# Forward attention scores as rows: q stationary in four column groups, K^T streamed 512 wide, softmax on rows, P transposed back

## The chip, the cores and the metric

The kernel runs on one core of a Trainium2 chip. The metric is device time in microseconds (us) of one execution; lower is better. The kernel before takes 2199 us (median of three executions, 2189 to 2205).

Names used below: PE is TensorE (matmuls), DVE is VectorE, ACT is ScalarE, POOL is GpSimd, PEld is the loading of stationary weights. PSUM is the memory that matmuls write, SBUF the working memory. The *granted clock* is the share of its full clock that PE had, as the profile records it. A *chunk* is eight transposed blocks of K, the content of one PSUM buffer. A *pair* is two heads of the attention that are worked on together. There are 128 heads (batch 4 times 32 heads), so 64 pairs.

## The reference, cut to what matters

A decode step of one attention block and one gated MLP, forward and backward. The part that matters is the attention forward, over a cache of 4096 keys of 128 numbers for each head:

```python
q = (x @ wq).reshape(B, Sq, H, Dh)...              # one query row per head
scores = jnp.einsum("bhqd,bhkd->bhqk", q, k_cache) * (Dh ** -0.5)
p = softmax(scores, axis=-1)
o = jnp.einsum("bhqk,bhkd->bhqd", p, v_cache)
# ... then the MLP, then the gradients of everything
# (cut: layer norms, MLP, vjp)
```

## The kernel before

Everything that the change touches lies in one stage, the forward over K and V. The engine order of each instruction queue is fixed when the kernel is built: the builder takes the operations in the order of the program as priorities, but lets a later operation go ahead where its inputs and buffers are ready in the builder's own estimate. Each queue then runs in that built order.

For one head, K is loaded with 32 rows of keys on each partition, PE transposes its 32 blocks (eight to a PSUM buffer, from a pool of two buffers, `psT`), and ACT and DVE copy them to `KT`. The scores are 32 matmuls with a block of K^T stationary and one column of q moving, so that the scores of a head fill a 128x32 tile:

```python
        def S_head(gi, hl):
            # ... cut: load of Kn, KT tile
            transpose_blocks(psT, KT, Kn, ["s", "v", "s", "s"])     # 4 chunks of 8 blocks; second chunk copied by VectorE
            # ...
            for j in range(SJ):
                nc.tensor.matmul(S_ps[:, hl, j:j + 1], lhsT=KT[:, j, :], rhs=qT_bf[:, bh:bh + 1], start=True, stop=True)
            hold[gi]["K"].append(Kn)

        def softmax(gi):
            S_ps = hold[gi]["S"]                                     # 128 x (2 heads x 32)
            nc.vector.tensor_reduce(out=mx[:], in_=S_ps[:], axis=AX.X, op=ALU.max)
            nc.tensor.transpose(xps[0:G, 0:P], mx[:], ident_f[:])    # maximum over partitions ...
            nc.vector.tensor_reduce(out=gm[:], in_=xps[0:G, 0:P], axis=AX.X, op=ALU.max)
            # ... cut: dg, and a small matmul that sends -scale*max to all partitions (bps, nm)
            for hl in range(G):
                nc.scalar.activation(out=E[:, hl, :], in_=S_ps[:, hl, :], func=AF.Exp, bias=nm[:, hl:hl + 1],
                                     scale=scale, accum_out=rs[:, hl:hl + 1])
            # ... cut: sum over partitions by a matmul with ones (lps), rl = 1 / sum
            nc.vector.tensor_tensor(out=P_all[:, gi * G:(gi + 1) * G, :], in0=E[:],
                                    in1=rl[:, :, None].to_broadcast([P, G, SJ]), op=ALU.mult)

        def M_head(gi, hl):
            # ... cut: load of Vn; PK = P x K, one product of 128x4096 on VectorE
            for j in range(SJ):
                nc.tensor.matmul(M_ps[:], lhsT=Vn[:, j, :], rhs=PK[:, j, :], start=(j == 0), stop=(j == SJ - 1))
            for c in range(2):                                       # kP: sums of PK over the keys, in four column groups
                for q in range(4):
                    # ...
                    nc.tensor.matmul(kP_ps[32 * q:32 * (q + 1), :, :], lhsT=ones_window(w), rhs=PK[:, j0:j0 + 4, 0:Dh],
                                     start=..., stop=..., tile_position=(0, 32 * q))
            # ... cut

        for gi in range(NGI + 1):
            if gi < NGI:
                for hl in range(G):
                    S_head(gi, hl)
                softmax(gi)
            if gi > 0:
                for hl in range(G):
                    M_head(gi - 1, hl)
```

Of the kernel before, what the change touches and what calls it, by code (L numbers as in the profile page):

```python
# [14 lines left out]
G = 2  # L15
# [10 lines left out]
def kernel(  # L26
# [71 lines left out]
    nc.vector.tensor_copy(out=sel_f[:], in_=ident_f[:, 0:H])  # L98
    for q in range(1, P // H):
        nc.vector.tensor_tensor(out=sel_f[:], in0=sel_f[:], in1=ident_f[:, q * H:(q + 1) * H], op=ALU.add)  # L100
    onesw = []
    for i in range(2):
        t = const.tile([P, 64], BF16, name=f"onesw{i}")
# [75 lines left out]
    def transpose_blocks(psW, XT, Xn, engs):  # L179
        for g in range(NG):  # L180
            pt = psW.tile([P, GW, P], BF16, tag="tps", name="pt_tps")
            for i in range(GW):
                nc.tensor.transpose(pt[:, i, :], Xn[:, g * GW + i, :], ident_b[:])  # L183
            evac_copy(XT[:, g * GW:(g + 1) * GW, :], pt[:], eng=engs[g % len(engs)])
# [38 lines left out]

    with ExitStack() as c1:
        psT = c1.enter_context(tc.tile_pool(name="psT", bufs=2, space=bass.MemoryType.PSUM))
        psS = c1.enter_context(tc.tile_pool(name="psS", bufs=2, space=bass.MemoryType.PSUM))
        psM = c1.enter_context(tc.tile_pool(name="psM", bufs=2, space=bass.MemoryType.PSUM))
        psK = c1.enter_context(tc.tile_pool(name="psK", bufs=1, space=bass.MemoryType.PSUM))
        psX = c1.enter_context(tc.tile_pool(name="psX", bufs=1, space=bass.MemoryType.PSUM))
# [1 line left out]
        xtp = c1.enter_context(tc.tile_pool(name="xtp", bufs=XT_BUFS))  # L231
        vp = c1.enter_context(tc.tile_pool(name="vp", bufs=V_BUFS))
        pkp = c1.enter_context(tc.tile_pool(name="pkp", bufs=PK_BUFS))
        wop = c1.enter_context(tc.tile_pool(name="wop", bufs=2))
        kps = c1.enter_context(tc.tile_pool(name="kps", bufs=1))
        hold = {}

        def S_head(gi, hl):
            bh = gi * G + hl
            b, h = bh_of(bh)  # L240
            Kn = kp.tile([P, SJ, Dh], BF16, name="Kn", tag="Kn")
            nc.sync.dma_start(out=Kn[:], in_=rows_of(A_k_cache[b, h]))
            KT = xtp.tile([P, SJ, P], BF16, name="KT", tag="KT")
            transpose_blocks(psT, KT, Kn, ["s", "v", "s", "s"])
            if hl == 0:
                hold[gi] = {"S": psS.tile([P, G, SJ], FP32, name="S_ps", tag="S"), "K": []}
            S_ps = hold[gi]["S"]
            for j in range(SJ):
                nc.tensor.matmul(S_ps[:, hl, j:j + 1], lhsT=KT[:, j, :], rhs=qT_bf[:, bh:bh + 1], start=True, stop=True)  # L249
            hold[gi]["K"].append(Kn)  # L250

        def softmax(gi):
            S_ps = hold[gi]["S"]
            mx = small.tile([P, G], FP32, tag="mx", name="mx")
            nc.vector.tensor_reduce(out=mx[:], in_=S_ps[:], axis=AX.X, op=ALU.max)  # L255
            xps = psX.tile([P, 512], FP32, tag="x", name="x_ps")
            nc.tensor.transpose(xps[0:G, 0:P], mx[:], ident_f[:])
            gm = small.tile([G, 1], FP32, tag="gm", name="gm")
            nc.vector.tensor_reduce(out=gm[:], in_=xps[0:G, 0:P], axis=AX.X, op=ALU.max)
            dg = small.tile([G, G], FP32, tag="dg", name="dg")  # L260
            nc.vector.tensor_scalar(out=dg[:], in0=ident_f[0:G, 0:G], scalar1=gm[:], scalar2=-scale,
                                    op0=ALU.mult, op1=ALU.mult)
            bps = psX.tile([P, 512], FP32, tag="x", name="b_ps")
            nc.tensor.matmul(bps[:, 0:G], lhsT=ones_f[0:G, :], rhs=dg[:], start=True, stop=True)
            nm = small.tile([P, G], FP32, tag="nm", name="nm")
            nc.vector.tensor_copy(out=nm[:], in_=bps[:, 0:G])
            E = small.tile([P, G, SJ], FP32, tag="E", name="E")
            rs = small.tile([P, G], FP32, tag="rs", name="rs")
            for hl in range(G):
                nc.scalar.activation(out=E[:, hl, :], in_=S_ps[:, hl, :], func=AF.Exp, bias=nm[:, hl:hl + 1],  # L270
                                     scale=scale, accum_out=rs[:, hl:hl + 1])
            lps = psX.tile([P, 512], FP32, tag="x", name="l_ps")
            nc.tensor.matmul(lps[:, 0:G], lhsT=ones_f[:], rhs=rs[:], start=True, stop=True)
            rl = small.tile([P, G], FP32, tag="rl", name="rl")
            nc.vector.reciprocal(out=rl[:], in_=lps[:, 0:G])
            nc.vector.tensor_tensor(out=P_all[:, gi * G:(gi + 1) * G, :], in0=E[:],
                                    in1=rl[:, :, None].to_broadcast([P, G, SJ]), op=ALU.mult)

        def M_head(gi, hl):
            bh = gi * G + hl  # L280
# [23 lines left out]
                                     start=(w == 0 and c == 0), stop=(w == 31 and c == 1), tile_position=(0, 32 * q))  # L304
            nc.scalar.copy(out=M_all[:, bh, :], in_=M_ps[:, 0:Dh + 1])  # L305
            if w == 31:
                kP_sb = kps.tile([P, 4, Dh], FP32, name="kP_sb", tag="kP_sb")
                nc.scalar.copy(out=kP_sb[:], in_=kP_ps[:])
                kt_ps = psX.tile([P, 512], FP32, tag="x", name="kt_ps")
                for c in range(4):  # L310
                    nc.tensor.matmul(kt_ps[:, 0:H], lhsT=kP_sb[:, c, :], rhs=sel_f[:], start=(c == 0), stop=(c == 3))
                nc.vector.tensor_copy(out=kPT[:, bh - 31:bh + 1], in_=kt_ps[:, 0:H])
# [409 lines left out]
```

## Time and profile before

| stage | from, us | to, us | what it does |
|---|---|---|---|
| forward | 20 | 944 | 64 pairs: transposes of K, scores, softmax, products with K and V |
| middle | 944 | 1102 | MLP forward and backward, small weights |
| backward | 1102 | 2202 | gradients of the caches, bound by DMA |

The table is read from the windows view (busy time of each engine in a stretch). The forward takes 924 us. In it PE's busy share is 0.87, DVE's 0.53, ACT's 0.49, and DMA's 0.75, so that no engine is full.

### The profile page before, as it was taken

How to read it: one execution, taken by the hardware profiler on the slowest of the kernel's cores; microseconds unless marked ns; L12 is line 12 of the kernel's file. 1: busy time of each engine (PE TensorE's matmuls, PEld its weight loads, DVE VectorE, ACT ScalarE, POOL GpSimd, SP SyncE). 2: the span in 40 equal slices, each digit the busy share in tenths (PEclk: the TensorE clock that was granted, in tenths of full speed). 3: DMA queues.
4: the chain of work that ended last, by engine and by line, in shares of the span. 5: the costliest groups of instructions: out<-in, count | busy, mean ns of one | idle time of the engine just before them, and what ended most of it. 6: DMA issues, size and time to landing. Idle time of an engine off the chain costs nothing.

```text
span 2202.3 us, 52207 instructions
## 1 busy us (share of the span) xinstructions
PE 1603.6 (73%) x23496; PEld 1321.8 (60%) x23496; DVE 1156.5 (53%) x1431; ACT 1074.7 (49%) x1523; POOL 212.7 (10%) x433
## 2 busy tenths in 40 slices
PE   7988888888888888868967798666556645465630
PEld 6777777777777767747956545555455545454530
DVE  3555555455545555533144455555566555565675
ACT  4555444454455444422267757565455544454520
POOL 0000000000000000000011111212112111111222
PEclk9999999999999999966568665555555555655555
DMA  8877777777777777633299999999999989999988
GB/s 332 325 298 305 300 289 290 290 311 311 286 285 291 309 288 286 256 130 135 72 397 371 407 351 380 394 385 400 389 390 380 373 344 400 353 376 362 382 344 341
DMA packets 110368, 710.74 MB, mean 323 GB/s; under 512 B 11568, under 2 KB 21624, under 8 KB 27712
## 3 DMA queue, kind: packets, MB, share of 16 engines
q1 hardware_dynamic: 66512, 418.94, 49.1%
q0 software_dynamic: 40704, 282.43, 31.5%
q10 hardware_dynamic: 2928, 6.03, 0.7%
q8 instruction: 184, 3.01, 0.5%
q14 instruction: 40, 0.33, 0.0%
HBM read 424.94 MB, written 282.34 MB: 321 GB/s over the span
## 4 chain that ended last, share of the span: by engine, by line
PE 33%; DMA 24%; DVE 17%; issue 15%; ACT 6%; POOL 4%; DVEq 0%; POOLq 0%; SPq 0%; ACTq 0%
DMA out_dram<-gk 20%; PE pt_tps L183 9%; PE M_ps L299 8%; DVE PK L288 6%; DVE gv L665 6%; PE kP_ps L303 4%; PE S_ps L249 4%; ACT KT L137 3%; PE dq_ps L557 2%; DVE gk L679 2%; ACT VT L137 2%; DMA V<-in_A_v_cache_dram 1%; POOL out_dram L671 1%; POOL P L663 1%; DMA out_dram<-gv 1%
## 5 line engine op out<-in xcount | busy, mean ns | idle before, releaser
L137 ACT COPY VT<-pt_tps 128x1024 bf16<-128x1024 bf16 x512 | 494.5, 1020 | 368.6 <-PE dP_ps L661 302.5
L183 PE MATMUL pt_tps<-ident_b,V 128*128 128x128 bf16 x4096 | 457.7, 285 | 147.7 <-ACT VT L137 129.2
L183 PEld LDWEIGHTS <-V 128*128 128x128 bf16 x4096 | 385.5, 131 | 209.3 <-issue 181.7
L137 ACT COPY KT<-pt_tps 128x1024 bf16<-128x1024 bf16 x384 | 376.9, 1014 | 240.5 <-PE pt_tps L183 239.4
L679 DVE TENSOR_TENSOR gk<-dS,rq 128x4096 bf16<-128x4096 bf16 x128 | 293.2, 2290 | 381.5 <-DMA out_dram<-gk 377.4
L183 PE MATMUL pt_tps<-ident_b,Kn 128*128 128x128 bf16 x4096 | 307.5, 225 | 13.4 <-ACT KT L137 9.4
L299 PE MATMUL M_ps<-PK,Vn 128*128 128x130 bf16 x4096 | 305.4, 221 | 3.0 <-DVE PK L287 2.5
L183 PEld LDWEIGHTS <-Kn 128*128 128x128 bf16 x4096 | 249.3, 100 | 93.3 <-issue 90.3
L665 DVE TENSOR_TENSOR gv<-P,rdo 128x4096 bf16<-128x4096 bf16 x128 | 292.2, 2283 | 6.9 <-DMA out_dram<-gv 4.7
L288 DVE TENSOR_TENSOR PK<-Kn,PK 128x4096 bf16<-128x4096 bf16 x128 | 293.4, 2292 | 3.8
L661 PE MATMUL dP_ps<-dOT_bf,VT 128*128 128x1 bf16 x4096 | 142.8, 166 | 193.1 <-DVE dSt L673 188.4
L661 PEld LDWEIGHTS <-VT 128*128 128x128 bf16 x4096 | 141.0, 104 | 212.3 <-issue 202.9
L299 PEld LDWEIGHTS <-Vn 128*128 128x128 bf16 x4096 | 252.7, 99 | 7.4 <-issue 5.7
L303 PE MATMUL kP_ps<-PK,onesw 128*32 128x512 bf16 x1024 | 119.1, 396 | 89.5 <-DVE PK L288 89.2
L249 PE MATMUL S_ps<-qT_bf,KT 128*128 128x1 bf16 x4096 | 165.9, 164 | 4.8 <-ACT KT L137 4.4
L249 PEld LDWEIGHTS <-KT 128*128 128x128 bf16 x4096 | 144.3, 96 | 29.8 <-ACT KT L137 23.7
L139 DVE COPY KT<-pt_tps 128x1024 bf16<-128x1024 bf16 x128 | 87.9, 687 | 123.4 <-PE pt_tps L183 123.4
L671 POOL DMA_DIRECT2D out_dram<-gv x128 | 68.4, 534 | 849.3 <-DVE dS L676 407.6
L305 ACT COPY M_all<-M_ps 128x129 f32<-128x129 f32 x128 | 34.3, 268 | 188.2 <-PE M_ps L299 187.9
L255 DVE TENSOR_REDUCE mx<-S_ps 128x2 f32<-128x64 f32 x64 | 14.4, 225 | 165.1 <-PE S_ps L249 165.1
L481 POOL DMA_DIRECT2D oflat_bf<-O_sb x4 | 2.1, 531 | 979.4 <-PE rep_ps L640 979.4
L685 POOL DMA_DIRECT2D out_dram<-gk x128 | 68.4, 534 | 96.9 <-DVE gk L679 84.5
(200 smaller groups left out, 1059.9 us busy)
## 6 DMA issues: line engine op xcount, KB each, us to landing
Kn<-in_A_k_cache_dram SPq DMA_DIRECT2D x128, 1024.0 KB, 8.8
Vn<-in_A_v_cache_dram SPq DMA_DIRECT2D x128, 1024.0 KB, 7.1
V<-in_A_v_cache_dram SPq DMA_DIRECT2D x128, 1024.0 KB, 9.7
out_dram<-gv POOLq DMA_DIRECT2D x128, 1024.0 KB, 9.1
out_dram<-gk POOLq DMA_DIRECT2D x128, 1024.0 KB, 13.8
wo<-in_A_wo_dram SPq DMA_DIRECT2D x16, 256.0 KB, 5.4
wq<-in_A_wq_dram SPq DMA_DIRECT2D x4, 1024.0 KB, 6.8
out_dram<-gst_wo POOLq DMA_DIRECT2D x8, 512.0 KB, 10.3
```

Of the source, the lines that this page charges most:

```text
L137: nc.scalar.copy(out=out_ap, in_=in_ap)
L139: nc.vector.tensor_copy(out=out_ap, in_=in_ap)
L183: nc.tensor.transpose(pt[:, i, :], Xn[:, g * GW + i, :], ident_b[:])
L249: nc.tensor.matmul(S_ps[:, hl, j:j + 1], lhsT=KT[:, j, :], rhs=qT_bf[:, bh:bh + 1], start=True, stop=True)
L288: nc.vector.tensor_tensor(out=PK[:, :, 0:Dh].rearrange("p j (r t) -> p j r t", t=2), in0=Kn.rearrange("p j (r t) -> p j r t", t=2), in1=PK ...
L299: nc.tensor.matmul(M_ps[:], lhsT=Vn[:, j, :], rhs=PK[:, j, :], start=(j == 0), stop=(j == SJ - 1))
L303: nc.tensor.matmul(kP_ps[32 * q:32 * (q + 1), :, :], lhsT=ones_window(w), rhs=PK[:, j0:j0 + 4, 0:Dh], start=(w == 0 and c == 0), stop=(w = ...
L661: nc.tensor.matmul(dP_ps[:, j:j + 1], lhsT=VT[:, j, :], rhs=dOT_bf[:, bh:bh + 1], start=True, stop=True)
L665: nc.vector.tensor_tensor(out=gv.rearrange("p j (r t) -> p j r t", t=2), in0=P2[:, :, None, :].to_broadcast([P, SJ, Dh // 2, 2]), in1=rdo[ ...
L671: nc.gpsimd.dma_start(out=rows_of(out_3[b, h]), in_=gv[:])
L679: nc.vector.tensor_tensor(out=gk.rearrange("p j (r t) -> p j r t", t=2), in0=dS2[:, :, None, :].to_broadcast([P, SJ, Dh // 2, 2]), in1=rq[ ...
L685: nc.gpsimd.dma_start(out=rows_of(out_2[b, h]), in_=gk[:])
```

## The change

The intent: the 32 one-column score matmuls of a head, each with a weight load, give way to eight matmuls that keep q stationary and stream K^T, 512 columns at a time. Each writes 32 rows of PSUM (two of them useful, one for each head of the pair), and four of them lie next to each other in the four column groups of the array. That takes some 5,000 instructions off PE. The price is that the scores now lie as rows of 1024 on all 128 partitions, so the softmax works on 128x1024, and P has to be transposed back to the layout in which the products use it.

```diff
-        psS = c1.enter_context(tc.tile_pool(name="psS", bufs=2, space=bass.MemoryType.PSUM))
+        psS = c1.enter_context(tc.tile_pool(name="psS", bufs=1, space=bass.MemoryType.PSUM))
 ... (cut: constants bsum, nscale, qwin; smaller SBUF pools, E and kP_sb in one buffer)
-            for j in range(SJ):
-                nc.tensor.matmul(S_ps[:, hl, j:j + 1], lhsT=KT[:, j, :], rhs=qT_bf[:, bh:bh + 1], start=True, stop=True)
+            for n in range(8):
+                u, c = n // 4, n % 4
+                nc.tensor.matmul(S_ps[32 * c:32 * (c + 1), u, :], lhsT=qwin[gi % 2][:, hl * 32:(hl + 1) * 32],
+                                 rhs=KT[:, 4 * n:4 * n + 4, :], start=(hl == 0), stop=(hl == G - 1), tile_position=(0, 32 * c))
 ...
-            nc.vector.tensor_reduce(out=mx[:], in_=S_ps[:], axis=AX.X, op=ALU.max)
+            nc.vector.tensor_reduce(out=mx[:], in_=S_ps.rearrange("p u k -> p (u k)"), axis=AX.X, op=ALU.max)
 ... (cut: gm over 512 elements on one partition; dg goes; nm)
+            nc.scalar.activation(out=E.rearrange("p u k -> p (u k)"), in_=S_ps.rearrange("p u k -> p (u k)"), func=AF.Exp,
+                                 bias=nm[:], scale=scale, accum_out=rs[:])
 ... (cut: lps with bsum, rl)
-            nc.vector.tensor_tensor(out=P_all[:, gi * G:(gi + 1) * G, :], in0=E[:],
-                                    in1=rl[:, :, None].to_broadcast([P, G, SJ]), op=ALU.mult)
+            nc.vector.tensor_scalar(out=Pn.rearrange("p s k -> p (s k)"), in0=E.rearrange("p u k -> p (u k)"),
+                                    scalar1=rl[:], scalar2=None, op0=ALU.mult)
+            pt = psT.tile([P, GW, P], BF16, tag="tps", name="pt_P")
+            for i in range(8):
+                nc.tensor.transpose(pt[:, i, :], Pn[:, i, :], ident_b[:])
 ... (cut: two copies of 128x32 from pt to P_all)
```

More of the change, by code (lines that the diff above doesn't have):

```diff
@@ L100 @@
         nc.vector.tensor_tensor(out=sel_f[:], in0=sel_f[:], in1=ident_f[:, q * H:(q + 1) * H], op=ALU.add)
+    bsum = const.tile([P, P], FP32, name="bsum")
+    nc.gpsimd.memset(bsum[:], 0.0)
+    for q in range(P // H):
+        for q2 in range(P // H):
+            nc.vector.tensor_copy(out=bsum[q * H:(q + 1) * H, q2 * H:(q2 + 1) * H],
+                                  in_=ident_f[q * H:(q + 1) * H, q * H:(q + 1) * H])
+    nscale = const.tile([1, 1], FP32, name="nscale")
+    nc.gpsimd.memset(nscale[:], -scale)
+    qwin = []
+    for i in range(2):
+        t = const.tile([P, G * 32], BF16, name=f"qwin{i}")
+        nc.gpsimd.memset(t[:], 0.0)
+        qwin.append(t)
     onesw = []
@@ L233 @@
         pkp = c1.enter_context(tc.tile_pool(name="pkp", bufs=PK_BUFS))
-        wop = c1.enter_context(tc.tile_pool(name="wop", bufs=2))
-        kps = c1.enter_context(tc.tile_pool(name="kps", bufs=1))
+        wop = c1.enter_context(tc.tile_pool(name="wop", bufs=1))
+        ep = c1.enter_context(tc.tile_pool(name="ep", bufs=1))
         hold = {}
@@ L243, in S_head @@
             KT = xtp.tile([P, SJ, P], BF16, name="KT", tag="KT")
+            if hl == 0:
+                nc.gpsimd.tensor_copy(out=qwin[gi % 2][:, 0:G * 32:33], in_=qT_bf[:, bh:bh + G])
+                hold[gi] = {"S": psS.tile([P, 2, 512], FP32, name="S_ps", tag="S"), "K": []}
             transpose_blocks(psT, KT, Kn, ["s", "v", "s", "s"])
-            if hl == 0:
-                hold[gi] = {"S": psS.tile([P, G, SJ], FP32, name="S_ps", tag="S"), "K": []}
             S_ps = hold[gi]["S"]
-            for j in range(SJ):
-                nc.tensor.matmul(S_ps[:, hl, j:j + 1], lhsT=KT[:, j, :], rhs=qT_bf[:, bh:bh + 1], start=True, stop=True)
+            for n in range(8):
+                u, c = n // 4, n % 4
+                nc.tensor.matmul(S_ps[32 * c:32 * (c + 1), u, :], lhsT=qwin[gi % 2][:, hl * 32:(hl + 1) * 32],
+                                 rhs=KT[:, 4 * n:4 * n + 4, :], start=(hl == 0), stop=(hl == G - 1), tile_position=(0, 32 * c))
             hold[gi]["K"].append(Kn)
@@ L253, in softmax @@
             S_ps = hold[gi]["S"]
-            mx = small.tile([P, G], FP32, tag="mx", name="mx")
-            nc.vector.tensor_reduce(out=mx[:], in_=S_ps[:], axis=AX.X, op=ALU.max)
+            mx = small.tile([P, 1], FP32, tag="mx", name="mx")
+            nc.vector.tensor_reduce(out=mx[:], in_=S_ps.rearrange("p u k -> p (u k)"), axis=AX.X, op=ALU.max)
             xps = psX.tile([P, 512], FP32, tag="x", name="x_ps")
-            nc.tensor.transpose(xps[0:G, 0:P], mx[:], ident_f[:])
-            gm = small.tile([G, 1], FP32, tag="gm", name="gm")
@@ L259, in softmax @@
-            nc.vector.tensor_reduce(out=gm[:], in_=xps[0:G, 0:P], axis=AX.X, op=ALU.max)
-            dg = small.tile([G, G], FP32, tag="dg", name="dg")
-            nc.vector.tensor_scalar(out=dg[:], in0=ident_f[0:G, 0:G], scalar1=gm[:], scalar2=-scale,
-                                    op0=ALU.mult, op1=ALU.mult)
-            bps = psX.tile([P, 512], FP32, tag="x", name="b_ps")
-            nc.tensor.matmul(bps[:, 0:G], lhsT=ones_f[0:G, :], rhs=dg[:], start=True, stop=True)
-            nm = small.tile([P, G], FP32, tag="nm", name="nm")
@@ L266, in softmax @@
-            nc.vector.tensor_copy(out=nm[:], in_=bps[:, 0:G])
-            E = small.tile([P, G, SJ], FP32, tag="E", name="E")
-            rs = small.tile([P, G], FP32, tag="rs", name="rs")
-            for hl in range(G):
-                nc.scalar.activation(out=E[:, hl, :], in_=S_ps[:, hl, :], func=AF.Exp, bias=nm[:, hl:hl + 1],
-                                     scale=scale, accum_out=rs[:, hl:hl + 1])
-            lps = psX.tile([P, 512], FP32, tag="x", name="l_ps")
-            nc.tensor.matmul(lps[:, 0:G], lhsT=ones_f[:], rhs=rs[:], start=True, stop=True)
@@ L274, in softmax @@
-            rl = small.tile([P, G], FP32, tag="rl", name="rl")
-            nc.vector.reciprocal(out=rl[:], in_=lps[:, 0:G])
-            nc.vector.tensor_tensor(out=P_all[:, gi * G:(gi + 1) * G, :], in0=E[:],
-                                    in1=rl[:, :, None].to_broadcast([P, G, SJ]), op=ALU.mult)
+            nc.tensor.transpose(xps[0:1, 0:P], mx[:], ident_f[:])
+            gm = ep.tile([1, 4, 32], FP32, tag="gm", name="gm")
+            nc.vector.tensor_reduce(
+                out=gm[:], in_=xps[0:1, 0:P].rearrange("o (c g) -> o g c", g=32)[:, None].to_broadcast([1, 4, 32, 4]),
+                axis=AX.X, op=ALU.max)
@@ new lines, in softmax @@
+            bps = psX.tile([P, 512], FP32, tag="x", name="b_ps")
+            nc.tensor.matmul(bps[:, 0:1], lhsT=gm.rearrange("o c g -> o (c g)"), rhs=nscale[:], start=True, stop=True)
+            nm = small.tile([P, 1], FP32, tag="nm", name="nm")
+            nc.vector.tensor_copy(out=nm[:], in_=bps[:, 0:1])
+            E = ep.tile([P, 2, 512], FP32, tag="E", name="E")
+            rs = small.tile([P, 1], FP32, tag="rs", name="rs")
+            nc.scalar.activation(out=E.rearrange("p u k -> p (u k)"), in_=S_ps.rearrange("p u k -> p (u k)"), func=AF.Exp,
+                                 bias=nm[:], scale=scale, accum_out=rs[:])
@@ new lines, in softmax @@
+            lps = psX.tile([P, 512], FP32, tag="x", name="l_ps")
+            nc.tensor.matmul(lps[:, 0:1], lhsT=bsum[:], rhs=rs[:], start=True, stop=True)
+            rl = small.tile([P, 1], FP32, tag="rl", name="rl")
+            nc.vector.reciprocal(out=rl[:], in_=lps[:, 0:1])
+            Pn = ep.tile([P, 8, P], BF16, tag="Pn", name="Pn")
+            nc.vector.tensor_scalar(out=Pn.rearrange("p s k -> p (s k)"), in0=E.rearrange("p u k -> p (u k)"),
+                                    scalar1=rl[:], scalar2=None, op0=ALU.mult)
@@ L279, in M_head @@
+            pt = psT.tile([P, GW, P], BF16, tag="tps", name="pt_P")
+            for i in range(8):
+                nc.tensor.transpose(pt[:, i, :], Pn[:, i, :], ident_b[:])
+            ptv = pt.rearrange("p (u jj) (c g) -> p g u c jj", jj=4, g=32)
+            for hl in range(G):
+                nc.vector.tensor_copy(out=P_all[:, gi * G + hl, :].rearrange("p (u c jj) -> p u c jj", u=2, c=4),
+                                      in_=ptv[:, hl])
         def M_head(gi, hl):
@@ L306, in M_head @@
             if w == 31:
-                kP_sb = kps.tile([P, 4, Dh], FP32, name="kP_sb", tag="kP_sb")
-                nc.scalar.copy(out=kP_sb[:], in_=kP_ps[:])
+                kP_sb = ep.tile([P, 8, Dh], FP32, name="kP_sb", tag="E")[:, 0:4, :]
+                nc.scalar.copy(out=kP_sb, in_=kP_ps[:])
                 kt_ps = psX.tile([P, 512], FP32, tag="x", name="kt_ps")
```

## The prediction

> **What bounds the kernel now.** I read the page's forty slices first, to see in which stage the changed lines live; then the windows view over one steady pair of heads; then the timeline of VectorE and of TensorE inside that pair; then the groups for durations.
>
> The slices:
>
> ```profile
> PE   7988888888888888868967798666556645465630
> DVE  3555555455545555533144455555566555565675
> ACT  4555444454455444422267757565455544454520
> DMA  8877777777777777633299999999999989999988
> ```
>
> Each digit is 55 us. Slices 1 to 17 are the forward over K and V (20 to 948 us, 64 pairs of heads, so (948 - 20) / 64 = 14.5 us a pair). There no engine is full: PE shows 8, DVE 5, ACT 4 or 5, DMA 7 (297 GB/s). From about 1100 us on is the backward, with DMA at 9. The change touches the forward alone; the other 1,270 us stay as they are.
>
> One pair, cut at its three parts (columns: busy time of PE, PEld, DVE, ACT, POOL with instruction counts, granted clock, DMA share, GB/s):
>
> ```profile
> 513.55:518.27 4.72, 2.85 (x51) 2.35 (x49) 4.69 (x4) 2.29 (x3) 0.00 (x0) 1.00 0.95 364
> 518.27:524.59 6.32, 6.18 (x127) 5.25 (x127) 1.29 (x3) 3.85 (x4) 0.00 (x0) 1.00 0.78 329
> 524.59:528.03 3.44, 3.44 (x50) 3.00 (x48) 1.28 (x7) 0.92 (x5) 0.00 (x0) 1.00 0.40 90
> ```
>
> The parts follow each other. First VectorE is full with the two products P x K (PK), PE waiting. Then PE, ScalarE and VectorE finish the transposes of the next pair and its scores. Then comes the softmax, in which VectorE works 1.28 of 3.44 us. VectorE's timeline of that pair shows what ties them:
>
> ```profile
> 513.55 2.29 DVE L288 TENSOR_TENSOR PK<-Kn,PK 128x4096 bf16<-128x4096 bf16 x1
> ...
> 515.98 2.29 DVE L288 TENSOR_TENSOR PK<-Kn,PK 128x4096 bf16<-128x4096 bf16 x1
> 518.19 0.68 DVE L139 COPY KT<-pt_tps 128x1024 bf16<-128x1024 bf16 x1
> 521.44 0.69 DVE L139 COPY KT<-pt_tps 128x1024 bf16<-128x1024 bf16 x1 [2.57 <-PE pt_tps L183]
> 524.59 0.23 DVE L255 TENSOR_REDUCE mx<-S_ps 128x2 f32<-128x64 f32 x1 [2.46 <-PE S_ps L249]
> 525.18 0.28 DVE L259 TENSOR_REDUCE gm<-x_ps 2x1 f32<-2x128 f32 x1 [0.36 <-PE x_ps L257]
> 525.49 0.22 DVE L261 TENSOR_SCALAR dg<-ident_f,gm 2x2 f32<-2x2 f32 x1
> 526.18 0.16 DVE L266 COPY nm<-b_ps 128x2 f32<-128x2 f32 x1 [0.47 <-PE b_ps L264]
> 527.49 0.17 DVE L275 RECIPROCAL rl<-l_ps 128x2 f32<-128x2 f32 x1 [1.16 <-PE l_ps L273]
> 527.77 0.23 DVE L276 TENSOR_TENSOR P_all<-E,rl 128x64 bf16<-128x64 f32 x1
> ```
>
> Brackets are idle time before the instruction. The next PK (528.26) stands behind P_all in VectorE's order, though it belongs to the pair before and needs nothing of this softmax; and the second chunk of a head's transposes is evacuated by VectorE behind PK. So the pair is a ring through VectorE: PK, PK, chunk copy, scores, softmax, PK. A longer softmax lengthens the ring unless something slides into its gaps.
>
> PE is second. I walked its timeline over the same pair and counted as idle only what it spends before an instruction: 0.83 and about 1.1 us before the column sums (kP) that wait for PK, and some 0.5 us in pieces. That leaves about 11.6 us of array work in 14.1 us. "8" is thus real work with some 2.5 us of slack.
>
> **What the Trainium skill says.** "TensorEngine Tiling (Array Packing)", section Instruction Overhead: a matmul with one moving column costs as much as one with 60. The trace agrees: 16 score matmuls last 0.54 us, one lasts 0.166, so (0.54 - 0.166) / 15 = 25 ns each. The same page, Key Properties: changing the tiling mode drains TensorE, and tiles run in parallel. kP is already in the form that the new scores take (32 columns stationary, 512 moving, four column groups): one lasts 0.39 us and eight last 0.61, so four run together and a second wave adds 0.22. "ScalarE: Activation LUTs", What ACT_TABLE_LOAD costs: an ACTIVATE with a pointer bias takes about 280 + 0.833 N ns; the trace has 283 ns at N = 32, a little under that. "VectorE: DVE Perf Modes", Why PSUM operands drop a tier: an fp32 operand in PSUM runs at 1x. The 4x512 and 128x56 copies from PSUM, 679 and 217 ns, give (679 - 217) / 456 = 1.01 ns per element, in agreement.
>
> **The change, part by part, per pair.**
>
> *Scores on PE.* Out: 64 matmuls of 25 ns = 1.6 us. In: 16 matmuls of 512. A chunk evacuation frees two of them, so they likely come in eight groups of two that run together: 0.215 us each. Around each lies a mode change. From kP in a stream of transposes I read its cost: 8 transposes start at 505.88, at 55 ns each they would end at 506.32, kP starts at 506.42 (0.10 lost); the two kP start there and the next transpose at 506.75, which is 0.33 and not 0.215 (0.115 lost). So 0.43 us a group, 8 x 0.43 = 3.4 us: PE gets 1.8 us more, not less. If the groups merge by four, 0.43 replaces 0.40 and it is even. So the intended saving doesn't appear in either case: one-column matmuls were at the issue floor, and streaming 512 columns of K^T takes the array the same time as the short ones.
>
> *Transposing P back.* 8 transposes at 55 ns: 0.45 us of PE. PE's sum is then about 11.6 + 1.8 + 0.45 = 13.9 us, or 12.1 if merged.
>
> *The softmax chain.* The tile grows from 128x64 to 128x1024, of which 2 of every 32 rows carry data; a row costs its length whatever it carries.
> - mx from PSUM: 225 ns at 64; plus 960 x 1.01 = 1.20 us: +0.97.
> - gm, 512 elements read instead of 128: 0.28 + 384 x 1.01 ns = 0.67: +0.39.
> - dg goes: -0.25 with its gap.
> - exp: two of 128x32 with their accumulator reads take 0.65 us from start to end; one of 1024 takes 0.283 + 992 x 0.833 ns = 1.11 and 0.1 for the rest of its read: +0.55.
> - Pn, tensor_scalar fp32 in SBUF to bf16: the 4x512 one (xhat, 533 ns) and the 4x1 one (141) give 0.77 ns per element, so about 0.9 us for 1024 (a 4x512 cast has 0.42, so it may be 0.7); it replaces P_all's 0.23: +0.6.
> - 8 transposes behind it: 0.61 as for 8 K transposes, plus 0.1 of hand-over: +0.7.
> - two copies of 32 elements into P_all, 0.19 each as for the 128x64 PK copy: +0.4.
>
> Sum: 0.97 + 0.39 - 0.25 + 0.55 + 0.6 + 0.7 + 0.4 = +3.4 us; the chain goes from 3.44 to about 6.8 us. VectorE's own work rises from 7.5 to about 9.6 us, ScalarE's from 7.1 to 7.6: neither becomes a bound.
>
> *Buffers.* The scores' PSUM goes from two buffers to one, so the next pair's first scores wait for this pair's exp; now they start 4 us after it, so this should stay hidden. P's transposes borrow one of the two buffers for K transposes, which holds back one chunk. DMA moves the same bytes; at 0.75 share it has room.
>
> **The rivals.**
>
> A. *Fully serial ring.* Nothing slides: 14.5 + 3.4 + some 0.2 for the last group of scores = 18.1 us a pair, 64 x 3.6 = +230 us: 2,430. For it: today's order of VectorE, in which PK stands behind P_all in spite of a gap of 1.16 us before rl. Against it: the order is fixed when the kernel is built and puts in what is ready; at 28.41 us a chunk copy does stand between gm and dg.
>
> B. *PK slides into the longer chain, PE binds.* PK's buffer comes free when the previous 64 M matmuls are done (3.65 us of PE, now spread over the softmax). In a chain of 6.8 us they end well before its end, so the first PK (2.5 us with its copy) can go into the gap at exp (about 1.7 us) or at the P transposes (0.7): 1.5 to 2 us come back. The pair is then 16.0 to 16.5 us, and PE with 13.9 us of work and today's 2.5 us of slack lands at the same place: 16.4. That is +1.5 to +2 us, +96 to +128 us: 2,295 to 2,327.
>
> C. *Everything overlaps.* The scores merge by fours, PE stays near 12.1, the gaps take PK and a chunk copy, and the ring stays at 14.5 or loses up to half a us: 2,165 to 2,200. Against it: an engine's order is strict, and three new handovers between VectorE and PE lie in the chain.
>
> D. *PE was the bound and is relieved* (the intent: 6,000 PE instructions go). It would need the scores' 1.6 us to vanish, some 100 us. The 25 ns pace and the mode changes speak against it.
>
> **Range and chances.** I put most weight on B, with a share of A as recovery will be partial: 16.6 us a pair, (16.6 - 14.5) x 64 = 134, so about 2,330 us. Low end: C at its slow side, 15.0 us, 2,225 or so; high end A, 2,430. Within 2% means under 2,243, a pair below 15.2 us: C or a good B, 0.2. Faster by 2% means under 2,155, a pair below 13.8 us, which is under my PE sum: 0.08. Slower: 0.72.
>
> **What would show it.** mx near 1.2 us, E near 1.1, Pn 0.7 to 0.9, gm 0.67; from the last score to P_all's last copy about 6.8 us or more; score matmuls of about 0.39 us in groups of two, with 0.1 us before and after; VectorE's busy share in the forward up from 53% to about 60%; PK standing between mx and P_all (B) or still behind P_all (A); backward unchanged near 1,100 us. I am wrong if PE's busy time in a pair falls with the pair, if the period is set by the single score buffer (a wait of score matmuls for E), or if the stage before the backward moves because memory is laid out anew.

## The result, and the profile after

The changed kernel takes 2368.7 us (median of four, 2367 to 2371), the kernel before 2202.2 us in the same rounds. The ratio is 1.077, with a 95% interval of 1.072 to 1.082: slower.

Where the time went is read from the windows view over the three stages, first of the kernel before (columns: length, then busy time and instructions of PE, PEld, DVE, ACT, POOL; granted clock, DMA share, GB/s):

```profile
20.00:944.15 924.15, 807.58 (x13669) 665.37 (x13666) 486.66 (x804) 454.22 (x772) 0.87 (x4) 0.98 0.75 294
944.15:1102.18 158.03, 132.45 (x1220) 113.59 (x1220) 40.82 (x87) 44.31 (x62) 4.78 (x9) 0.61 0.34 116
1102.18:2202.30 1100.12, 656.65 (x8463) 536.39 (x8460) 624.93 (x527) 573.09 (x685) 204.82 (x407) 0.58 0.95 376
```

and of the changed kernel:

```profile
20.00:1101.60 1081.60, 932.34 (x11106) 664.80 (x11104) 601.37 (x867) 485.02 (x644) 12.83 (x66) 0.93 0.69 251
1101.60:1259.70 158.10, 132.36 (x1220) 114.24 (x1220) 40.84 (x87) 44.29 (x62) 4.77 (x9) 0.61 0.34 115
1259.70:2365.10 1105.40, 656.33 (x8463) 537.79 (x8460) 624.86 (x527) 572.55 (x685) 205.78 (x407) 0.58 0.94 374
```

The forward is 157 us longer, the middle the same, the backward 5 us longer. PE's busy time in the forward went up by 125 us although it has 2,563 matmuls fewer. And its granted clock fell from 0.98 to 0.93, which the prediction had not named.

DVE's timeline of one pair after the change, in the place of the one that the prediction shows:

```profile
512.46 1.22 DVE L272 TENSOR_REDUCE mx<-S_ps 128x1 f32<-128x1024 f32 x1 [2.98 <-PE S_ps L264]
514.08 0.68 DVE L276 TENSOR_REDUCE gm<-x_ps 1x128 f32<-1x512 f32 x1 [0.40 <-PE x_ps L274]
515.23 0.16 DVE L282 COPY nm<-b_ps 128x1 f32<-128x1 f32 x1 [0.47 <-PE b_ps L280]
517.16 0.17 DVE L290 RECIPROCAL rl<-l_ps 128x1 f32<-128x1 f32 x1 [1.77 <-PE l_ps L288]
517.44 0.75 DVE L292 TENSOR_SCALAR Pn<-E,rl 128x1024 bf16<-128x1024 f32 x1
518.90 0.29 DVE L299 COPY P_all<-pt_P 128x32 bf16<-128x32 bf16 x2 [0.71 <-PE pt_P L296]
519.13 0.30 DVE L310 COPY PK<-P_all 128x64 bf16<-128x64 bf16 x2
519.37 2.29 DVE L311 TENSOR_TENSOR PK<-Kn,PK 128x4096 bf16<-128x4096 bf16 x1
521.58 0.68 DVE L152 COPY KT<-pt_tps 128x1024 bf16<-128x1024 bf16 x1
522.18 2.28 DVE L311 TENSOR_TENSOR PK<-Kn,PK 128x4096 bf16<-128x4096 bf16 x1
```

From the start of `mx` to the first copy for PK it is 519.13 - 512.46 = 6.67 us. PK still stands behind P_all, and no other DVE work has slid into the gaps of the softmax.

I cut every pair of both traces at three points on DVE: from the start of `mx` to the start of the first product PK, its copies included (chain), from there to the end of the second PK (products), and from there to the next `mx` (rest of the scores). The means over 63 pairs, worked out from the timelines:

| | chain | products | rest of the scores | pair |
|---|---|---|---|---|
| before | 3.76 | 5.06 | 5.53 | 14.35 |
| after | 7.13 | 5.13 | 4.53 | 16.79 |
| difference | +3.37 | +0.07 | -1.00 | +2.44 |

2.44 x 64 = 156 us, the growth of the forward. This table describes the loss; it does not yet say that the chain's length causes it.

Two more readings of the traces correct the picture with which I predicted. First, to which pair does PK belong? DVE's timeline at the start of the kernel before answers it:

```profile
27.61 0.23 DVE L255 TENSOR_REDUCE mx<-S_ps 128x2 f32<-128x64 f32 x1 [2.78 <-PE S_ps L249]
...
32.58 0.23 DVE L276 TENSOR_TENSOR P_all<-E,rl 128x64 bf16<-128x64 f32 x1
...
33.10 2.35 DVE L288 TENSOR_TENSOR PK<-Kn,PK 128x4096 bf16<-128x4096 bf16 x1
...
35.97 2.28 DVE L288 TENSOR_TENSOR PK<-Kn,PK 128x4096 bf16<-128x4096 bf16 x1
39.34 0.23 DVE L255 TENSOR_REDUCE mx<-S_ps 128x2 f32<-128x64 f32 x1 [1.09 <-PE S_ps L249]
```

This is the very first softmax, and both PK follow it before the second softmax starts. So PK behind P_all is the product of the same pair, which needs that P_all. The program text puts M_head one pair later, but the builder has pulled it forward. PK could therefore never slide ahead of its own softmax; what can slide beside the softmax is the *next* pair's transposes.

Second, where did the 1.00 us in the rest of the scores come back? In the kernel before, PE's queue has the column sums kP between the transposes, where they wait for PK; after the change they come later. The group of kP before:

```profile
L303 PE MATMUL kP_ps<-PK,onesw 128*32 128x512 bf16 x1024 | 119.1, 396 | 89.5 <-DVE PK L288 89.2
```

and after (columns: busy us, mean ns | idle before them, ended by):

```profile
L326 PE MATMUL kP_ps<-PK,onesw 128*32 128x512 bf16 x1024 | 81.4, 388 | 0.0
```

89 us of waiting, 1.4 us a pair, are gone. That this is the 1.00 us is an argument from two numbers, not an experiment.

The clock: most pairs of the changed kernel last about 16.0 or about 17.1 us, some in between and a few 18 to 19.5. A long one and a short one, in the windows view:

```profile
62.78:79.84 17.06, 14.77 (x174) 10.72 (x173) 9.22 (x13) 7.53 (x10) 0.19 (x1) 0.90 0.67 247
230.12:246.13 16.01, 14.10 (x176) 9.63 (x175) 9.90 (x16) 7.53 (x10) 0.19 (x1) 1.00 0.77 279
```

Inside the long one, in stretches of 2 us, the clock (third number from the end) is 1.00 except in two:

```profile
66.78:68.78 2.00, 0.59 (x6) 0.51 (x7) 0.92 (x2) 0.39 (x3) 0.00 (x0) 1.00 0.85 291
68.78:70.78 2.00, 2.00 (x24) 2.00 (x22) 1.39 (x5) 0.48 (x1) 0.00 (x0) 0.53 0.67 279
70.78:72.78 2.00, 1.70 (x16) 1.11 (x15) 2.00 (x3) 0.90 (x2) 0.00 (x0) 0.62 0.00 0
```

In the 2 us before the fall PE was busy for 0.59 us only: it waited 0.54 us for exp and 1.12 us for Pn. In the short pair a small matmul (`at_ps`, once in four pairs) happens to lie in that gap. The Trainium skill, "TensorE: Matmul & The Clock Gate", section "HAM oscillation — how this bites in real kernels", tells of the clock falling when PE idles over some 3.4 us, and in its next section, "A second HAM failure mode: psum-queue depth-cycling", of micro-idles that do the same. This trace is nearer to the second: no gap here comes near 3.4 us.

The gaps alone do not decide it, though. In 51 pairs both (at least 0.54 and 1.05 us) stand with nothing but the small matmul `l_ps` between them; in 36 of these the clock fell, in 15 it did not (these last 16.09 us each), and it also fell in 3 of the 12 pairs with `at_ps` in the gap. In the clock records of this trace the falls start at whole multiples of 3.413 us from one another and most last 3.41 us, so it seems to matter also how the gaps lie on that grid. No run tests this.

### The profile page after: what moved, and what is told of

It is laid out like the page before. It is cut to its first block, busy times and chain, and to the rows that moved or that the text cites. A ratio compares the mean times of both kernels' runs of the same rounds, so it can differ in the third digit from the quotient of the medians.

```text
span 2365.1 us, 47165 instructions
## 1 busy us (share of the span) xinstructions
PE 1728.2 (73%) x20936; PEld 1323.5 (56%) x20936; DVE 1273.2 (54%) x1511; ACT 1104.9 (47%) x1395; POOL 226.2 (10%) x501
## 4 chain that ended last, share of the span: by engine, by line
PE 38%; DMA 22%; issue 14%; DVE 13%; ACT 8%; POOL 4%; DVEq 0%; ACTq 0%; POOLq 0%; SPq 0%
DMA out_dram<-gk 19%; PE pt_tps L196 11%; PE M_ps L322 10%; PE S_ps L264 6%; DVE gv L688 5%; ACT E L285 3%; ACT KT L150 3%; DVE PK L311 2%; PE dq_ps L580 2%; DVE Pn L292 2%; PE pt_P L296 2%; PE kP_ps L326 2%; ACT VT L150 1%; DVE gk L702 1%; POOL P L686 1%
## 5 line engine op out<-in xcount | busy, mean ns | idle before, releaser
L196 PE MATMUL pt_tps<-ident_b,Kn 128*128 128x128 bf16 x4096 | 351.3, 238 | 33.8 <-ACT KT L150 33.8
L322 PE MATMUL M_ps<-PK,Vn 128*128 128x130 bf16 x4096 | 338.2, 224 | 10.3 <-DVE PK L311 10.3
L196 PEld LDWEIGHTS <-Kn 128*128 128x128 bf16 x4096 | 283.8, 108 | 97.6 <-issue 91.6
L322 PEld LDWEIGHTS <-Vn 128*128 128x128 bf16 x4096 | 257.6, 99 | 99.7 <-issue 98.0
L272 DVE TENSOR_REDUCE mx<-S_ps 128x1 f32<-128x1024 f32 x64 | 78.4, 1225 | 190.9 <-PE S_ps L264 190.9
L264 PE MATMUL S_ps<-KT,qwin 128*32 128x512 bf16 x1024 | 179.7, 397 | 0.7 <-ACT KT L150 0.7
L285 ACT ACTIVATE E<-S_ps,nm 128x1024 f32<-128x1024 f32 x64 | 71.2, 1113 | 158.0 <-DVE nm L282 157.9
L258 POOL COPY qwin<-qT_bf 128x2 bf16<-128x2 bf16 x64 | 12.3, 193 | 1020.6 <-PE S_ps L264 1006.0
L296 PE MATMUL pt_P<-ident_b,Pn 128*128 128x128 bf16 x512 | 47.8, 248 | 60.1 <-DVE Pn L292 58.6
L326 PE MATMUL kP_ps<-PK,onesw 128*32 128x512 bf16 x1024 | 81.4, 388 | 0.0
```

The lines of the kernel that those rows point to most:

```text
L196: nc.tensor.transpose(pt[:, i, :], Xn[:, g * GW + i, :], ident_b[:])
L264: nc.tensor.matmul(S_ps[32 * c:32 * (c + 1), u, :], lhsT=qwin[gi % 2][:, hl * 32:(hl + 1) * 32], rhs=KT[:, 4 * n:4 * n + 4, :], start=(hl ...
L285: nc.scalar.activation(out=E.rearrange("p u k -> p (u k)"), in_=S_ps.rearrange("p u k -> p (u k)"), func=AF.Exp, bias=nm[:], scale=scale, ...
L296: nc.tensor.transpose(pt[:, i, :], Pn[:, i, :], ident_b[:])
```

## The experiments

The theory that I began with, from the prediction: the pair is a ring through DVE, and a longer chain is paid in full (**ring**). The first rival: PE's work of some 13.7 us in the strict order of its queue sets the pair, and the change's mode switches and transposes are the loss (**TensorE**). The runs below brought in two more: that the **clock** falls, and that the **built order** decides how much lies beside the softmax.

### 1. A shorter maximum

```diff
-  in_=S_ps.rearrange("p u k -> p (u k)")
+  in_=S_ps[:, 0, :]                          # one half; any shift gives the right softmax here
```

> The changed kernel with the maximum taken over one of the two halves of the scores (the result stays right: any shift does). Only mx gets shorter, from 1.22 to about 0.70 us. Ring theory (scores, softmax and the P x K products follow each other through VectorE, so the softmax chain is paid in full): 0.52 x 64 = 33 us less than the changed kernel, about 2335. TensorE theory (its 13.7 us of work in the strict order of its queue set the pair): no change, about 2369.

Measured: 2303.7 us, ratio to before 1.044 (1.039 to 1.050). That is 65 us less than the changed kernel, twice what the ring theory allowed. The pairs now last 15.6 us almost without exception, where the changed kernel has 16.0 to 17.1, and the granted clock over the stretch from 100 to 900 us is 0.99 in place of 0.93. So about 0.5 us a pair is the shorter `mx` (16.1 to 15.6), as the ring says, and the rest is the clock. The expectation missed because it left the clock out. The trace also shows why the clock held: the builder moved two kP matmuls into PE's gap in 60 of the 64 pairs (none in the changed kernel):

```profile
519.79 0.40 PE L326 MATMUL kP_ps<-PK,onesw 128*32 128x512 bf16 x2
520.99 0.62 PE L296 MATMUL pt_P<-ident_b,Pn 128*128 128x128 bf16 x8 [0.80 <-DVE Pn L292]
```

Between 40 us and the last `mx` the clock fell 4 times, against 38 in the changed kernel, and 3 of the 4 falls (at 301, 554 and 807 us) stand at pairs without those two kP.

### 2. No maximum at all

```diff
-  mx, xps, gm, bps, nm (all of them)
-  nc.scalar.activation(..., bias=nm[:], scale=scale, accum_out=rs[:])
+  nc.scalar.activation(..., scale=scale, accum_out=rs[:])
```

> The changed kernel without the maximum and all that broadcasts it (exp of the scaled scores directly; right for these small scores). The chain loses the stretch from mx's start to nm's end, 2.93 us of 6.67. Ring theory: 64 x 2.93 = 187 us less, about 2180. TensorE theory: only the two small matmuls go, 0.4 us a pair, about 2340. A result near 2180 would also say that the new form of the scores costs nothing beside the longer chain, as the chain is then about the length of the kernel before.

Measured: 2207.6 us, ratio 1.001 (0.996 to 1.007), 161 us less than the changed kernel. Nearer to the ring (187) than to TensorE (26). But the clock is 1.00 here, and run 5 below puts the clock at some 30 us, so about 130 of the 187 us are left for the chain. That split is an argument: the builder reordered here too, with 16 M matmuls between `l_ps` and the transposes of P in most pairs and kP waiting 25 us for PK (0 in the changed kernel). The result also says that with a softmax of about the old length, in this build, the new scores and the transposes of P cost nothing that shows.

### 3. The kernel before with a chain as long as the change's

```diff
-  nc.vector.tensor_reduce(out=mx[:], in_=S_ps[:], axis=AX.X, op=ALU.max)
+  nc.vector.tensor_reduce(out=mx[:], in_=S_ps[:, :, None, :].to_broadcast([P, G, 51, SJ]), axis=AX.XY, op=ALU.max)
```

> The kernel before with its mx read 51 times over (same result), so that the chain is 3.2 us longer, as much as the change made it, with TensorE's work as before. Ring theory: the loss of the change comes back, +2.4 us a pair, +150 us, about 2350 (up to +205 if nothing slides). TensorE theory (the loss is the 1.8 us of mode changes and the transposes of P): under half of it, at most +80.

Measured: 2168.4 us, ratio 0.983 (0.977 to 0.990). The kernel got *faster*, by 34 us (clear of no change, not clear of 2%), with `mx` at 3.56 us in place of 0.23:

```profile
505.68 3.56 DVE L255 TENSOR_REDUCE mx<-S_ps 128x2 f32<-128x3264 f32 x1
```

This is the result that felled the ring theory as I had put it. There is no wait in brackets: the scores were ready when the products ended. Over the trace (the 61 pairs of 63 with two PK) the chain is 7.53 us (before 3.76), the products 5.06, and the rest of the scores 1.15 (before 5.53); all pairs together average 13.8. The builder, seeing a longer `mx`, had put the next pair's first transposes and a chunk copy beside the softmax, and most of the kP elsewhere in PE's queue: kP's waiting for PK is 2.6 us in all, 89 before. In this built order the longer chain thus cost nothing, with the next pair's transposes beside it.

### 4. The score matmuls twice

```diff
+  for each group of two: the same two matmuls with lhsT=zero32 (zeros), accumulated
```

> The changed kernel with each score matmul issued a second time with a stationary of zeros, accumulated (same result). TensorE gets at least 16 x 0.215 / 2 = 1.7 us more work a pair, next to the old, with no more mode changes; the chain stays. TensorE theory: 64 x 1.7 = +110 us over the changed kernel, about 2480. Ring theory: only the last group's wave lies ahead of mx, +0.2 us a pair, and some of the rest while VectorE has its products: +15 to +40, about 2390 to 2410.

Measured: 2348.7 us, ratio 1.066 (1.061 to 1.071), 20 us *less* than the changed kernel with 16 more matmuls a pair. TensorE's work as the bound is out. Most pairs last 16.3 us, which is the 0.2 us more of the ring theory over a pair at full clock (16.1), and the clock is 0.99: it fell 3 times in place of 38. As in run 1 the builder had moved kP matmuls (three) into PE's gap in 60 of 64 pairs. So it need not be the added work itself that kept the clock up; the expectation missed its sign because it left the clock out.

### 5. Only the clock

```diff
+            warm = psX.tile([P, 512], FP32, tag="x", name="warm_ps")
+            for i in range(3):
+                nc.tensor.matmul(warm[:], lhsT=ident_b[:], rhs=hold[gi]["K"][0][:, 4 * i:4 * i + 4, :], start=True, stop=True)
             Pn = ep.tile([P, 8, P], BF16, tag="Pn", name="Pn")
```

> The changed kernel with three matmuls of 512 columns, whose result nobody reads, in TensorE's idle stretch between l_ps and the transposes of P. The built order of every engine is otherwise that of the changed kernel. In the changed kernel's trace pairs last 16.0 us at a granted clock of 1.00 or 17.1 us at 0.90, the clock falling to 0.53 for some 3.4 us just after that idle stretch. Clock theory: the extra work keeps the clock, all pairs go to about 16.05 us, 64 x (16.79 - 16.05) = 47 us less, about 2320. Rival (the low clock is a consequence of waiting and costs nothing): no change, 2369, or a little more.

Measured in five rounds: 2333.6 us, ratio 1.056 (1.053 to 1.059). The extra work made the kernel 35 us faster by the medians, 46 by the two ratios to before. PE's timeline shows it in the gap, and the clock line of the slices is at 9 for the whole forward:

```profile
66.69 0.38 PE L288 MATMUL l_ps<-rs,bsum 128*128 128x1 f32 x2 [0.55 <-ACT E L285]
67.33 0.81 PE L293 MATMUL warm_ps<-Kn,ident_b 128*128 128x512 bf16 x3 [0.26 <-DVE rl L290]
68.20 0.62 PE L299 MATMUL pt_P<-ident_b,Pn 128*128 128x128 bf16 x8
```

```profile
PEclk9999999999999999996657766555555565556555
```

The same line of the changed kernel:

```profile
PEclk8989989999989889997657766655555555555555
```

The clock fell twice in place of 38 times. The chain and the products are as long as in the changed kernel (7.13 and 5.13); only the rest of the scores went from 4.53 to 4.09, and the pair from 16.79 to 16.34. The expected 16.05 holds for most pairs (16.1), not for the mean. Apart from the added matmuls the built order of every queue is the changed kernel's, but for `at_ps` and a few operations around it, which stand some places apart in 12 of the 64 pairs. So this run shows the clock's share of the loss: 35 us by the medians, 46 by the ratios, 0.45 x 64 = 29 us by the pairs. "Some 30 us" below is rounded from these.

### 6. A bank of its own for the transposes of P

```diff
-            pt = psT.tile([P, GW, P], BF16, tag="tps", name="pt_P")
+            pt = psX.tile([P, GW, P], BF16, tag="x", name="pt_P")
```

> The changed kernel with the transposes of P in the small matmuls' PSUM bank instead of the pool of the K transposes (one word). The built order now has 15 transposes of the next pair before them (none before), and a chunk copy of K inside the chain on VectorE. Theory now: the lengthened chain costs what it does because the P transposes, in the pool of the K transposes, keep the next pair's transposes behind it, and because TensorE, idle there, falls to a lower clock in part of the pairs (0.93 granted in the forward). So two chunks (0.9 us of PE, one copy of 0.93 us on ScalarE and one of 0.69 on VectorE) leave the stretch after PK, and the clock goes back to 0.98 or more: 1.5 to 2.2 us a pair less, about 2230 to 2275. Rival (the chain's own length is paid whatever lies beside it, and only the clock was lost): 16.1 us a pair, about 2325.

Measured: 2214.6 us, ratio 1.005 (1.001 to 1.010): of the 167 us lost, one word gives back 154. It came out 15 us better than the better end of what was expected. PE's timeline around the transposes of P in this kernel:

```profile
526.95 0.38 PE L288 MATMUL l_ps<-rs,bsum 128*128 128x1 f32 x2
527.19 1.00 PE L196 MATMUL pt_tps<-ident_b,Kn 128*128 128x128 bf16 x15
528.45 0.62 PE L296 MATMUL pt_P<-ident_b,Pn 128*128 128x128 bf16 x8 [0.26 <-DVE Pn L292]
```

and in the changed kernel:

```profile
516.74 0.38 PE L288 MATMUL l_ps<-rs,bsum 128*128 128x1 f32 x2 [0.54 <-ACT E L285]
518.25 0.62 PE L296 MATMUL pt_P<-ident_b,Pn 128*128 128x128 bf16 x8 [1.12 <-DVE Pn L292]
518.71 1.43 PE L196 MATMUL pt_tps<-ident_b,Kn 128*128 128x128 bf16 x16
```

In the changed kernel, and in runs 1, 2, 4 and 5, no transpose of the next pair precedes those of P within a softmax, in any of the 64 pairs. With the own bank some do in 63 pairs, 16 or more in 52, and in the pair shown PE's wait for Pn shrinks from 1.12 to 0.26 us. The means over the 61 pairs with two PK: chain 7.25, products 4.95, rest of the scores 2.24; all pairs together average 14.41. The chain is as long as in the changed kernel, even a little longer; the 2.3 us come out of the rest. The clock is 1.00, with 2 falls, so the 154 us contain the clock's share of run 5; the two do not add.

The one word changed much of PE's and DVE's built order besides this, so the run shows what the shared pool cost in all, not each step of how. It also bounds a rival that no run tests alone: the change's smaller SBUF pools are still in this kernel, which is within 1% of the kernel before.

### 7. The same with a shorter maximum

> The kernel of a_own_bank with the maximum over one half of the scores, mx 0.53 us shorter. If the chain is still paid in full once the next pair's transposes run beside it: 34 us less than a_own_bank, about 2180. If TensorE's 13.9 us of work in its order now sets the pair: no change, 2205 to 2215.

```diff
-  in_=S_ps.rearrange("p u k -> p (u k)")          # on top of run 6
+  in_=S_ps[:, 0, :]
```

Measured: 2230.7 us, ratio 1.010 (1.008 to 1.012): no gain over run 6 (1.005; the intervals overlap, so a loss is not shown) though the chain is shorter, and outside both expectations. The chain did get shorter (6.61 against 7.25), but the rest of the scores grew from 2.24 to 3.15. The builder had ordered the queues anew; that this took back the 0.5 us is likely, not shown.

### 8. M_head ahead of the softmax, in the kernel before

```diff
                     S_head(gi, hl)
-                softmax(gi)
             if gi > 0:
                 for hl in range(G):
                     M_head(gi - 1, hl)
                 del hold[gi - 1]
+            if gi < NGI:
+                softmax(gi)
```

> The kernel before with M_head of the previous pair written ahead of the softmax of this pair: the same instructions, another built order (TensorE does the 64 M matmuls and kP before x_ps, and 14 transposes of the next pair between x_ps and l_ps; one chunk copy lies in the softmax on VectorE). Theory (a pair costs the softmax chain, the two PK and what of the scores is left after them; the order decides how much is left): the rest after PK falls from 5.5 to 1 or 2 us while the chain grows a little, 12.5 to 13 us a pair against 14.35, about 2090 to 2120. Rival (the order does not matter, TensorE's or VectorE's work does): 2200.

Measured: 2173.5 us, ratio 0.987 (0.983 to 0.991), 31 us less, a third of what was expected. The rest of the scores fell to 1.28 us, as said. But the chain grew to 7.63, more than the "little" of the expectation: all 64 M matmuls now stand ahead of the small transpose of the maximum in PE's queue, and `gm` waits 179 us in all for it (25 before).

### 9. M_head right after the scores of its head

```diff
                     S_head(gi, hl)
+                    if gi > 0:
+                        M_head(gi - 1, hl)
                 softmax(gi)
```

> The kernel before with each M_head written right after the scores of a head. Built order: l_ps, 7 transposes, 32 scores, 12 transposes, then M. Same theory: better than before, 12.5 to 13.5 us a pair, 2090 to 2150; but the 32 M of the first head stand ahead of the second head's scores and wait for the first PK, so it may be behind b_products_first.

Measured: 2197.2 us, ratio 0.997 (0.993 to 1.001): no gain; outside the range expected, though behind run 8 as said. The rest of the scores is 4.00, the chain 5.54, and the granted clock from 100 to 900 us is 0.91. I did not follow it further.

### 10 to 12. Shorter softmaxes, and combinations

Run 10 takes the maximum out of the kernel before, as run 2 does with the changed one:

```diff
-  mx, xps, gm, dg, bps, nm (all of them)
-  nc.scalar.activation(..., func=AF.Exp, bias=nm[:, hl:hl + 1], ...)
+  nc.scalar.activation(..., func=AF.Exp, ...)
```

> The kernel before without the maximum and its broadcast: the chain is 1.75 us shorter, and nothing else is meant to change. If the chain's length is paid: 64 x 1.75 = 112 us less, about 2090. If the order decides: the built order has no transposes of the next pair before P_all and both chunk copies after the two PK, so little is gained, 2150 to 2200.

Measured: 2170.4 us, ratio 0.985 (0.981 to 0.989): 34 us less, where 112 would have been the chain's length paid. In this build kP still waits 99 us for PK.

Run 11 adds to it the edit of run 8:

```diff
-  softmax(gi) ahead of the two M_head(gi - 1, hl)
+  softmax(gi) behind them
```

> The kernel before without the maximum and with M_head of the previous pair written first. Each alone gave about 30 us. If the two add: 2140. The built order though has 32 M and only then transposes after l_ps, so that the gain of b_products_first (transposes of the next pair inside the softmax) is not there: 2165 to 2180 then.

Measured: 2171.2 us, ratio 0.983 (0.980 to 0.985), as expected from its built order: the two gains do not add.

Run 12 puts runs 2, 6 and 8 together on the changed kernel:

```diff
-  mx, xps, gm, bps, nm;  pt from psT;  softmax(gi) ahead of M_head(gi - 1, hl)
+  exp without a bias;    pt from psX;  softmax(gi) behind them
```

> The changed kernel with the own bank for P's transposes, without the maximum, M_head of the previous pair first: 16 transposes of the next pair directly after l_ps in the built order. The chain is 2.9 us shorter than in a_own_bank; if two thirds of that are paid, 64 x 1.9 = 120 us less, about 2090 to 2110, and it beats both kernels. If TensorE's work (about 13.5 us a pair here) sets it: 2150 to 2170.

Measured: 2197.2 us, ratio 0.994 (0.990 to 0.998), above both expectations; a pair is 14.1 us. What sets it there I did not find.

Several builds of quite different kinds (runs 3, 8, 10 and 11) end at 2168 to 2174 us, that is at 13.7 to 13.9 us a pair. What that level is made of stays open. Of the kernels that compute the full softmax, runs 3 and 8 beat both kernels, run 8 by 1.3% and 8% with a change of the order in the program alone. Runs 10 and 11 are as fast but drop the maximum, which is right only where scores are small.

## Why the prediction was right or wrong

The time, 2369 us, lies between the low end (2,225 or so) and the high end (2,430) that were given, 39 us above the 2,330 in the middle, and "slower" had a chance of 0.72. The costs of the softmax's parts were right; that their sum landed so near was in part luck, as the steps show.

**Scores on PE: right.** No saving appeared. The groups of one to four take 0.32 to 0.34 us from their start to the next matmul, with some 0.1 us lost ahead of them, as read from kP before. They merged in part: seven groups a pair in place of eight. The new matmuls last 397 ns on average, predicted 390. Some 5,100 PE instructions went, where rival D counts 6,000. Run 4 shows that this work is not what the pair waits for: with 16 more matmuls a pair is 16.44 us on average, against 16.34 in run 5, both at nearly full clock.

**The softmax chain: right in its terms.** `mx` 1.22 us (predicted 1.20), `gm` 0.68 (0.67), exp 1.11 (1.11), Pn 0.75 (0.7 to 0.9), Pn to P_all 0.71 (0.71), the whole 6.67 in the pair shown (6.8).

**"...though it belongs to the pair before and needs nothing of this softmax": wrong.** PK is the product of the same pair. So rival B's reason, that PK slides into the longer chain, could not happen, and did not: PK stands behind P_all in every pair, which is the sign that the prediction had named for A. B's number, 16.4 us a pair, was nonetheless near the 16.79 measured. That is luck: 1.0 us came back in another place, probably on PE, where kP no longer stood between the transposes waiting for PK (89 us in all; the link is argued above, not tested).

**"P's transposes borrow one of the two buffers for K transposes, which holds back one chunk": the term that was mis-sized.** It was taken as a detail and given no time. In the built order they held back all of the next pair's transposes until after the softmax, and run 6 puts it at 154 us, the clock's share included: nearly the whole loss.

**The ring, "a longer softmax lengthens the ring unless something slides into its gaps": right only with its second half.** Run 3 lengthened `mx` by 3.3 us and was faster; run 6 kept the long chain and was within 1% of the kernel before. Runs 1 and 2 got back the chain's length in full and to some two thirds (the clock's share taken off), both in builds where the next pair's transposes stayed behind P's. In these runs the loss needs the long chain *and* the transposes locked out of it. The builder reordered in each of them, so no run changes one of the two with all else fixed.

**The clock: not in the prediction at all.** After PE's two gaps in the longer softmax its clock fell in most pairs. Run 5 measures 29 to 46 us for it. I had predicted PE's idle time there and asked only what could fill it, not what it does to the clock.

**The last paragraph: half right.** The backward is unchanged (1105 us against 1100), no score matmul waits for the single score buffer (0.7 us in all, put down to ACT's copies of KT), and the middle did not move. DVE's busy share in the forward rose from 53% to 56%, where 60% was expected, as the forward got longer too.

## What to carry to other kernels

Before you add an operation to a chain, look where its buffer comes from: a small late step that draws on the pool of a large early stage can lock the next iteration's early work behind it, and that can cost more than the step. When a queue's order is fixed at build time, the length of a chain tells little by itself; ask what stands beside it in each queue, and test by moving one buffer or one call before reasoning in durations. And treat an idle gap on TensorE as a possible cost to the matmuls behind it: look at the granted clock, since here filling the gap with useless work already paid (run 5).

## What the Trainium skill lacked or had wrong

- "TensorE: Matmul & The Clock Gate", section "HAM oscillation — how this bites in real kernels", gives the rule as no gaps over some 3.4 us; its next section, on micro-idles, gives no length. Here the clock fell to 0.53 (in a 2 us slice) after gaps of 0.54 and 1.12 us with little between them (PE busy 0.59 of 2.00 us), in 36 of the 51 pairs that have both, at a cost of some 0.5 to 1 us each; three useless matmuls of 0.81 us together removed nearly all falls (run 5, 38 to 2).
- The same page, "Part 4: PE-mode transpose", says that a transpose does not raise the clock and takes some 275 ns in a kernel. One lasts 225 ns on average in the forward before, but in a stream sixteen last 1.05 us and eight 0.61, so a further one adds (1.05 - 0.61) / 8 = 55 ns. From 68.89 to 72.30 us of the changed kernel PE ran transposes alone at a clock of 0.50, and from then on the clock was 1.00. The trace does not name the mode of these transposes.
- "TensorEngine Tiling (Array Packing)", Key Properties, says that a change of tiling mode drains TensorE, without a figure. Here about 0.1 us is lost going into four column groups and 0.115 us coming out (estimates, worked out in the prediction from the starts at 505.88, 506.42 and 506.75 us in the kernel before).
- "ScalarE: Activation LUTs" has no figure for reading the accumulator after an exp: a separate instruction of 0.19 us, of which about 0.1 us shows.
- No page that I read says that a shared pool of PSUM buffers can fix the order of two stages in the built queues; here it cost 154 us (run 6).
